# One Strassen chain for the 512 tokens of a block instead of two plain rows and a chain for 256

## The chip, the core and the metric

The kernel runs on one core of a Trainium2 chip. The metric is the device time in microseconds; the times of before are those of 3 runs. All other times here come from one profiled execution.

## What is computed

Attention over 8 batches of 8 heads, 576 positions and 64 channels, with a bias that depends on the distance, and on its output a two-layer block with a snake activation:

```python
scores = scale * np.matmul(q, k.transpose(0, 1, 3, 2)) + bias
attn = softmax(scores)                              # over the last axis
x = np.matmul(attn, v)  # heads side by side: 4608 tokens x 512
h = x @ w_in                                        # 512 -> 2048
s = np.sin(alpha * h)
g = h + s * s / (alpha + 1e-09)
out = g @ w_out                                     # 2048 -> 512, float32
```

## The kernel before

A planner in the kernel's own code orders everything. Each step is a `Task` with the engines that may take it, an assumed duration, its dependencies, a priority and the buffers that it uses; `Plan.run` places the steps one after another by these assumed times and emits their instructions in that order. On the chip each engine then runs its instructions strictly in that order and waits on semaphores for data and for buffers. The planner knows when a step on an engine ends; it does not know how long a store to memory takes: the store is issued inside the step that writes its buffer, and the buffer counts as free when that step ends.

The 4608 tokens are worked in 9 blocks of 512. While batch `t` is in attention (scores and attention outputs on TensorE, exp on ScalarE, the bias as a mask product on VectorE), the second layer of an earlier block is dealt out among its matmuls as filler (`fill`, with the quotas `QUOTA`, `QUOTA1`, `OFFSET`). Then comes the first layer of block `t` (`plan_moe_in`: 64 matmuls of 512 columns; sine on ScalarE, square on ScalarE or VectorE, `g` on VectorE), and then the attention of batch `t + 1`. ScalarE loads a table for exp and one for sine at each change.

The second layer of a block has three forms. Block 0 has four plain rows of 128 tokens (`plan_mo`: 16 matmuls of 512 columns into one bank, a copy to an `outs` buffer and a store of 256 KB). Blocks 1 to 6 have two plain rows and, for the other 256 tokens, a chain (`plan_chain`): a 2 x 2 Strassen product in Winograd's form, with seven products of 8 matmuls of 256 columns, four sums of `g` quarters on VectorE (s1 to s4, in four pieces each; s3 and s4 go to `ss` or over `g` itself) and combined weights in `wsum`. Products share banks by twos. Their results are put together in `outs` by a copy `x` and adds named c11, y, v, w, c22, c21 and c12 after what they make: `take`, line 1389. Blocks 7 and 8 at the end are done by `plan_half`.

Two things matter for what follows. First, buffers: the `outs` tiles are a ring (`NBUF["outs"]`), and a new one may be written only once the store of its last content has landed. PSUM has eight banks: scores and the first layer use 0 to 5, attention outputs (`av`) and second-layer rows and products (`mo`) use 6 and 7. Second, the DMA queues: stores, and the transposes that bring attention outputs to `xT`, are issued by SP in one order; GpSimd issues loads of `v` and, for a batch two later, copies of `k` and `q` in 16 bits to memory (`stage_kq`, from `staged_k` and `staged_q`), which are loaded transposed by SP one block later. Those copies have 576 KB each in small pieces, and `to_stage` puts them at the first layer of blocks 1 to 5.

```python
NBUF = {"ut": 2, "ss": 1, "u": 2, "g": 2, "s16": 3, "sq": 3, "outs": 5, "xn": 6}
BANKS = {"h": (0, 1, 2, 3, 4, 5), "av": (6, 7), "mo": (7, 6), "st": (7, 6, 0, 1, 2, 3, 4, 5)}
```

Of the kernel before, what the change touches and what calls it, by code (L numbers as in the profile page):

```python
# [222 lines left out]

WINDOW = 700
WARM_END = 22.0
QUOTA = 47
QUOTA1 = 28
OFFSET = 0
T_START = 4.0
STEPS = {0: ((1, 1, 1, 1),) * 3, 1: ((3, 1),) * 3}  # L230
T_W0 = 24.5
PRI_S = 0
T_WI = 16.8
# [14 lines left out]
P_ST = 3  # L248
T_TP = ((150, 150), (650, 650), (1500, 1500))
GA = 0.0  # L250
GB = 0.0
GUARD = {"A": GA, "B": GB, "C": 0.0, "X": 0.0}
T_LD = 33.0

AV_AT = (3, 4, 6, 7)
AV_D = (0, 0, 300, 0)
AV_G = (3, 7)
PRE = -100
CUT = 8
RUNS = "aaa c aaa aaa aaa c x aaa abb"  # L260
TAKE = 0
MOEP = (5, 25)
STEP = 700
MIX = "nnssss"
SUMS = {1: (0, 1, 2, 3)}
PACE = ((0, 0), (0, 0), (2, 1), (8, 1))
T_WS = (43.0, 48.3, 48.3, 48.3)
MIX0 = "nnssss"
FIRST = 1
CH = ("mo", "mo", "mo", "st")  # L270
PIECES = 4
AV_LATE = 9900
AV0 = 1500
FILL_GAP = 0.05
# [8 lines left out]
WARM_LAG = 0.3  # L283
WARM_GAP = 0.12
WARM_FROM = 7.3
AV_PRI = 0
NORM_PRI = 200
CP_PRI = 0
SIN_SET = "trig_and_small"
SLACK = {"PE": 0.02, "ACT": 0.02, "DVE": 0.02, "POOL": 0.02, "SP": 0.02}  # L290
# [14 lines left out]
def kernel(  # L305
# [75 lines left out]

    xT = sgl.tile([128, NP, XN], F16, name="xT")
    wsum = sgl.tile([128, 4, NF // 2, DM // 2], F16, name="wsum")
    xv = zz


    natx = tp.tile([128, NF * DM], F16, name="natx", tag="g", bufs=2)
# [26 lines left out]
        return tp.tile([128, DM], F16, name="sq", tag="sq", bufs=NBUF["sq"])  # L414

    def new_ss():
        return tp.tile([128, 6, 512], F16, name="ss", tag="ss", bufs=NBUF["ss"])
# [668 lines left out]
    def plan_moe_in(b, tbl):  # L1086
# [5 lines left out]
        for f in range(NF):  # L1092
# [3 lines left out]
            def mm(e, js, f=f, h=h, hb=hb):  # L1096
                if js[0] == 0:
                    h.v = bank(hb)
                x0 = 512 * b % XN
                m = min(512, XN - x0)  # L1100
                for y, a, n in ((0, x0, m), (m, 0, 512 - m)):
                    if n == 0:
                        continue
                    for j in js:
                        full(h.v[:, y : y + n], w_in16[:, j, 128 * f : 128 * f + 128],
                             xT[:, j, a : a + n], j == 0, j == 3)

            def sn(e, f=f, h=h, s16=s16):
                s16.v = new_s16()
# [52 lines left out]
    def plan_mo(b, a, cut=NF):  # L1162

        mb, ob, m = Buf("mo"), Buf("outs"), Cell()
        for f in range(NF):
            if f == cut:
                yield

            def mm(e, f=f):
                if f == 0:  # L1170
                    m.v = bank(mb)
                full(m.v, gcell[b].v[:, f, 128 * a : 128 * a + 128], w_out16[:, f, :], f == 0, f == NF - 1)

            mo_last[:] = [plan.add({"PE": t_pe(DM)}, mm, mo_last[:] + [gdone[(b, f)]],
                                   500000000 + 4 * b + a, nb=T_WO[f // 4] if b == 0 else 0.0,
                                   new=[mb] if f == 0 else [],
                                   use=[gbuf[b]] if f == 0 else [gbuf[b], mb])]
            mo_last[0].fill = True

        def cp(e):  # L1180
            o = new_outs()
            copy_on(e, o, m.v)
            r0 = 512 * b + 128 * a
            nc.sync.dma_start(out=out[r0 : r0 + 128], in_=o)
# [31 lines left out]
    def plan_half(b, a):  # L1216
# [65 lines left out]
        def add(k, j, to, deps, put=None, first=False, c0=0, c1=n):  # L1282

            def ad(e):
# [2 lines left out]
                    return  # L1287
                cell, i, h = to
                if first:
                    cell.v = new_outs()  # L1290
# [28 lines left out]
    def plan_chain(b, a):  # L1319

        H2, n = NF // 2, DM // 2
        sv, sb = Cell(), Buf("ss")
        bk = [Buf(x) for x in CH]
        bv = [Cell() for _ in range(4)]
        o = Cell(), Cell()
        ob = Buf("outs"), Buf("outs")
        gall = [gdone[(b, f)] for f in range(NF)]
        base = 500000000 + 4 * b + a

        def act(i, j):  # L1330
            return gcell[b].v[:, H2 * j : H2 * j + H2, 128 * (a + i) : 128 * (a + i) + 128]

        def pre(out, x, y, op, deps, first=False):

            made = []
            for h in range(PIECES):
                r = slice(H2 // PIECES * h, H2 // PIECES * (h + 1))

                def sm(e, h=h, r=r):
                    if first and h == 0:  # L1340
                        sv.v = new_ss()
                    nc.vector.tensor_tensor(out=out()[:, r], in0=x()[:, r], in1=y()[:, r], op=op)

                new = first and h == 0
                made.append(plan.add({"DVE": 0.07 + 0.533 / PIECES}, sm, deps + made[-1:], base + PRE, new=[sb] if new else [],
                                     use=[gbuf[b]] if new else [sb, gbuf[b]]))
            return made[-1]

        def sums(k):
            return sv.v[:, 2 * k : 2 * k + 2].rearrange("p k (f t) -> p (k f) t", f=H2 // 2)  # L1350

        def at(k):
            return bv[k // 2].v[:, n * (k % 2) : n * (k % 2) + n]

        def put(i, j):
            if i == 2:
                return xv.bitcast(F32)
            return o[i].v[:, n * j : n * j + n]

        def prod(k, x, w, deps):  # L1360

            for f in range(H2):

                new = f == 0 and k % 2 == 0

                def mm(e, f=f, new=new):
                    if new:
                        bv[k // 2].v = bank(bk[k // 2])
                    full(at(k), x()[:, f], w()[:, f], f == 0, f == H2 - 1)

                mo_last[:] = [plan.add({"PE": t_pe(n)}, mm, mo_last[:] + deps, base,
                                       new=[bk[k // 2]] if new else [],
                                       use=([] if new else [bk[k // 2]]) + [sb, gbuf[b]])]
                mo_last[0].fill = True
                mo_last[0].part = n / DM
                mo_last[0].bank, mo_last[0].reads = bk[k // 2], False
            return mo_last[0]

        def wq(i, j):
# [3 lines left out]
            return lambda: wsum[:, k]  # L1383

        def store(i):
            r = 512 * b + 128 * (a + i)
            nc.sync.dma_start(out=out[r : r + 128, :], in_=o[i].v)

        def take(k, to, x, deps, new=False, last=False):

# [1 line left out]

            def ev(e):
                if new:
                    o[i].v = new_outs()
                if x is None:
                    copy_on(e, put(i, j), at(k))
                else:
                    nc.vector.tensor_tensor(out=put(i, j), in0=at(k), in1=put(*x), op=ALU.add)
                if last:  # L1400
                    store(i)

            bs = [sb] if i == 2 else [] if new else [ob[i]]
            y = plan.add({"DVE": t_dve(n)} if x else {"ACT": t_act(n), "DVE": t_dve(n)}, ev, deps, TAKE,
                         new=[ob[i]] if new else [], use=[bk[k // 2]] + bs)
            y.bank, y.reads = bk[k // 2], True
            return y
# [4 lines left out]
        s4 = pre(lambda: sums(2), lambda: act(0, 1), lambda: sums(1), ALU.subtract, [s2])  # L1412
        p = prod(0, lambda: act(0, 0), wq(0, 0), gall)
        x = take(0, (2, 0), None, [p])
        p = prod(1, lambda: act(0, 1), wq(1, 0), [])
        c11 = take(1, (0, 0), (2, 0), [p, x], True)
        yield
        p = prod(2, lambda: sums(1), ws(1), [s2] + wdone)
        y = take(2, (1, 1), (2, 0), [p, x], True)
        p = prod(3, lambda: act(1, 0), ws(2), [s3])  # L1420
        v = take(3, (1, 0), (1, 1), [p, y])
        yield
        prod(4, lambda: act(1, 1), ws(3), [])
        p = prod(5, lambda: sums(0), ws(0), [])
        w = take(5, (0, 1), (1, 1), [p, y])
        c22 = take(5, (1, 1), (1, 0), [p, v, w])
        take(4, (1, 0), (1, 0), [p, v, c22], last=True)
        yield
        p = prod(6, lambda: sums(2), wq(1, 1), [s4])
        take(6, (0, 1), (0, 1), [p, w, c11], last=True)  # L1430
# [16 lines left out]
    for t in range(T):  # L1447
# [39 lines left out]
            sins += s_  # L1487
        pe_gate = [m]
        if t < T - 1:
            rows = [plan_mo(t, a, CUT if t == 0 and a < 2 else NF) for a in range(2 if t >= FIRST else 4)]  # L1490
            if t == 0 and CUT < NF:
                next(rows[0])
                next(rows[1])
            if t >= FIRST:
                rows, ch = iter(rows), plan_chain(t, 2)
                for x in MIX if t else MIX0:
                    next(next(rows) if x == "n" else ch)
            else:
                for x in rows:
                    next(x)  # L1500
# [38 lines left out]
```

## Time and profile before

| | |
|---|---|
| median of 3 runs | 364.72 us (363.8 to 364.89) |
| profiled execution | 363.98 us, span 362.0 us |
| granted TensorE clock | 0.999 |
| busy: TensorE, ScalarE, VectorE, GpSimd | 356.1, 316.5, 307.0, 93.4 us |
| moved by DMA | 40.53 MB |

The span runs from the first to the last instruction. Busy is the time in which an engine had at least one instruction in work; matmuls overlap in it, so the mean of a matmul's record is longer than the step from one to the next. In rows of a timeline the columns are start, duration, engine, line, operation, what is written from what, shapes and count; in square brackets is the idle time ahead of it and what ended it. SPq is SP's own queue: its rows are the issue of a DMA, not its transfer. Rows of DMA groups give count, size of one and the median time from issue to landing; the answer for one tile and a short window gives the landing of the DMAs issued in it. Of the DMA queues, `software_dynamic` are those that GpSimd issues and `hardware_dynamic` those of SP.

### The profile page before, as it was taken

The numbers are of one execution on the slowest core, as the hardware profiler recorded it, in microseconds if no ns is written. First come the engines' busy times: TensorE is split into PE (matmuls) and PEld (weight loads), VectorE is DVE, ScalarE is ACT, GpSimd is POOL, SyncE is SP. The second block draws the span as 40 slices with busy tenths as digits, with TensorE's granted clock in tenths as the row PEclk, the third lists the DMA queues.
The fourth block names the chain that finished last, engine by engine and source line by source line (L and its number), as shares of the span: only waits on it lengthen the run. The fifth ranks groups of instructions, "written<-read, shape, count | busy, mean of one in ns | idle before, by whom it ended". The sixth has DMA issues, their size and how long they took to land.

```text
span 362.0 us, 9625 instructions
## 1 busy us (share of the span) xinstructions
PE 356.1 (98%) x3812; PEld 218.3 (60%) x3812; DVE 307.0 (85%) x757; ACT 316.5 (87%) x437; POOL 93.4 (26%) x135
## 2 busy tenths in 40 slices
PE   8999999999999999999999999999999999999996
PEld 4564445644575447885684458545787467456685
DVE  4897888989977998699978997899869986999982
ACT  2998999989998999899989999899989998996811
POOL 8578460064000820065001900092006000000000
PEclk9999999999999999999999999999999999999999
DMA  9999999689824996199918992599339422001023
GB/s 169 199 197 183 206 162 144 127 91 123 115 60 104 129 150 109 50 167 140 136 26 167 113 170 51 117 142 144 90 76 151 73 61 53 17 2 59 31 75 102
DMA packets 150157, 40.53 MB, mean 112 GB/s; under 512 B 137224, under 2 KB 145504, under 8 KB 150112
## 3 DMA queue, kind: packets, MB, share of 16 engines
q0 software_dynamic: 96064, 17.67, 60.5%
q1 hardware_dynamic: 53872, 22.16, 25.9%
q8 instruction: 30, 0.49, 0.5%
q10 hardware_dynamic: 176, 0.09, 0.1%
q14 instruction: 15, 0.12, 0.1%
HBM read 37.73 MB, written 16.56 MB: 150 GB/s over the span
## 4 chain that ended last, share of the span: by engine, by line
PE 94%; DMA 2%; DVE 1%; ACT 1%; issue 0%; DVEq 0%; SPq 0%
PE pb L497 92%; DMA m2r<-e_dram 1%; DVE u L779 1%; ACT u L748 1%; DMA e_dram<-e_sb 1%; PE pb L597 1%; PE pb L1066 1%; ACT e_sb L646 0%; PE pb L591 0%; DVE xn L995 0%; ACT xT L578 0%; DVE outs L1292 0%; DVE zz L548 0%; DVE u L765 0%; DVE rd L994 0%
## 5 line engine op out<-in xcount | busy, mean ns | idle before, releaser
L748 ACT ACTIVATE u<-pb 128x1024 f16<-128x1024 f32 (+1 forms) x146 | 136.9, 1018 | 6.3 <-PE pb L497 5.1
L497 PE MATMUL pb<-xT,w_in 128*128 128x512 f16 (+4 forms) x704 | 128.6, 340 | 0.3 <-ACT xT L578 0.3
L1124 DVE SCALAR_TENSOR_TENSOR g<-sq,inv_a,pb 128x512 f16<-128x512 f16 x144 | 101.4, 744 | 3.8 <-ACT sq L1117 1.8
L1110 ACT ACTIVATE s<-pb,alphaT 128x512 f16<-128x512 f32 x144 | 92.9, 693 | 12.4 <-PE pb L497 11.6
L497 PEld LDWEIGHTS <-w_in 128*128 128x128 f16 x704 | 64.4, 98 | 55.5 <-issue 0.5
L497 PE MATMUL pb<-w_out,g 128*128 128x512 f16 (+1 forms) x416 | 83.5, 339 | 0.0
L497 PEld LDWEIGHTS <-g 128*128 128x128 f16 x552 | 50.8, 98 | 34.8 <-issue 5.2
L779 DVE TENSOR_TENSOR u<-u,m2r 128x512 f16<-128x512 f16 (+1 forms) x128 | 61.9, 491 | 9.9 <-ACT u L748 8.5
L497 PEld LDWEIGHTS <-u 128*128 128x128 f16 x1280 | 56.0, 97 | 9.1 <-issue 4.5
L1117 ACT ACTIVATE sq<-s 128x512 f16<-128x512 f16 x76 | 47.5, 640 | 2.0 <-DVE g L1124 1.1
L442 POOL COPY kt<-kT 64x256 f16<-64x256 f16 x12 | 4.9, 406 | 168.9 <-DMA kT<-staged_k 140.6
L497 PE MATMUL pb<-v,u 128*128 128x65 f16 x1024 | 43.9, 193 | 0.0
L497 PE MATMUL pb<-qT,kT 64*128 64x64 f16 (+1 forms) x512 | 42.1, 285 | 0.7 <-DVE qT L580 0.3
L1119 DVE TENSOR_TENSOR sq<-s 128x512 f16<-128x512 f16 x68 | 28.3, 424 | 11.3 <-ACT s L1110 10.3
L995 DVE TENSOR_TENSOR xn<-pb,rd 128x256 f16<-128x256 f32 (+2 forms) x59 | 28.5, 483 | 2.0
L497 PEld LDWEIGHTS <-kT 64*128 64x128 f16 x512 | 17.1, 94 | 20.5 <-issue 13.1
L497 PE MATMUL pb<-vh,u 128*128 128x130 f16 x128 | 28.3, 221 | 0.0
L447 POOL DMA_DIRECT2D v<-in_v_dram x28 | 24.7, 892 | 3.2 <-DMA nat<-in_k_dram 2.2
L1437 ACT ACT_TABLE_LOAD x15 | 19.2, 1283 | 0.3
L748 ACT ACTIVATE nat<-pb 128x1024 f16<-128x1024 f32 (+1 forms) x24 | 18.8, 820 | 0.0
L994 DVE RECIPROCAL rd<-pb 128x4 f32<-128x4 f32 (+2 forms) x59 | 10.9, 185 | 8.1 <-PE pb L497 7.0
L497 PE MATMUL pb<-wsum,g 128*128 128x256 f16 (+1 forms) x136 | 16.7, 267 | 0.0
(96 smaller groups left out, 310.9 us busy)
## 6 DMA issues: line engine op xcount, KB each, us to landing
out_dram<-outs SPq DMA_DIRECT2D x28, 256.0 KB, 2.8
v<-in_v_dram POOLq DMA_DIRECT2D x28, 128.0 KB, 4.7
staged_k<-in_k_dram POOLq DMA_DIRECT2D x6, 576.0 KB, 8.7
staged_q<-in_q_dram POOLq DMA_DIRECT2D x6, 576.0 KB, 12.5
w_in<-in_moe_w_in_dram POOLq DMA_DIRECT2D x4, 512.0 KB, 9.2
w_out<-in_moe_w_out_dram POOLq DMA_DIRECT2D x4, 512.0 KB, 13.6
out_dram<-outs SPq DMA_DIRECT2D x16, 128.0 KB, 1.7
w_out<-in_v_dram SPq DMA_DIRECT2D x6, 128.0 KB, 5.5
```

Source lines behind the costliest of these rows:

```text
L442: nc.gpsimd.tensor_copy(out=kts[t % 2][r, :, r], in_=kTs[t % 2][r, :, 512:S])
L447: nc.gpsimd.dma_start(out=vs[t % 2][:, c, :, 0:D], in_=vp[128 * c : 128 * c + 128],)
L497: nc.tensor.matmul(out=out, lhsT=lhsT, rhs=rhs, start=start, stop=stop, skip_group_check=go_on)
L748: nc.scalar.activation(out=o, in_=x, func=AF.Exp, scale=0.125)
L779: nc.vector.tensor_tensor(out=io, in0=io, in1=m2[:, 2 * p : 2 * p + 2, x0 : x0 + hi - lo], op=ALU.mult)
L994: nc.vector.reciprocal(out=r, in_=x[:, :, :, D])
L995: nc.vector.tensor_tensor(out=xn[:, 0:n].rearrange("p c (z d) -> p c z d", z=2), in0=x[:, :, :, 0:D], in1=r.unsqueeze(3).to_broadcast([128 ...
L1110: nc.scalar.activation(out=s16.v, in_=h.v, func=AF.Sin, scale=alphaT[:, f : f + 1])
L1117: nc.scalar.activation(out=sq.v, in_=s16.v, func=AF.Square)
L1119: k_of(e).tensor_tensor(out=sq.v, in0=s16.v, in1=s16.v, op=ALU.mult)
L1124: nc.vector.scalar_tensor_tensor(out=gcell[b].v[:, f, :], in0=sq.v, scalar=inv_a[:, f : f + 1], in1=h.v, op0=ALU.mult, op1=ALU.add,)
L1437: nc.scalar.preload_act_table_set(name)
```

## The change

- From block 1 to block 6 the second layer is one chain for all 512 tokens: seven products of 16 matmuls of 256 columns, each filling a whole bank (two groups of 128 tokens beside each other). The two plain rows of these blocks go. The order of the products is 0, 1, 2, 3, 5, 4, 6.
- All products take their bank from 6 and 7 (`CH`). The last product is not put into a bank of its own: it is added by TensorE onto the sixth's (`ONTO`), so that the add w falls away.
- The sums are of twice the size, in two pieces instead of four; s4 now overwrites a quarter of `g`. Adds and copies have 512 columns in one instruction (128 x 2 x 256). The copy `x` goes straight into the second half of an `outs` tile.
- An `outs` tile is twice as large and holds 256 tokens, its store has 512 KB, and the ring has 2 tiles instead of 5. `plan_mo` and `plan_half` use half a tile of the same ring. `ss` grows from 6 to 8 pieces.
- The first three feature groups of each block's first layer are split (3, 1) over the four channel groups (`STEPS`); before, only in blocks 0 and 1.
- The planner's quotas, priorities and assumed durations for squares are others.

```diff
-NBUF = {"ut": 2, "ss": 1, "u": 2, "g": 2, "s16": 3, "sq": 3, "outs": 5, "xn": 6}
+NBUF = {"ut": 2, "ss": 1, "u": 2, "g": 2, "s16": 3, "sq": 3, "outs": 2, "xn": 6}
...
-QUOTA = 47
+QUOTA = 34
...
-CH = ("mo", "mo", "mo", "st")
-PIECES = 4
+CH = ("mo",) * 7
+ONTO = True
+ACC = False
+ORD = (0, 1, 2, 3, 5, 4, 6)
+XE = {"ACT": 0.479, "DVE": 0.603}
+PIECES = 2
...
-SQ = {"ACT": 0.51, "DVE": 0.355}
+SQ = {"ACT": 0.45, "DVE": 0.4}
...
     def new_outs():
-        return tp.tile([128, DM], F32, name="outs", tag="outs", bufs=NBUF["outs"])
+        return tp.tile([128, 2 * DM], F32, name="outs", tag="outs", bufs=NBUF["outs"])
...
-        def prod(k, x, w, deps):
+        def prod(k, x, w, deps, onto=None):
 
-            for f in range(H2):
+            z = k if onto is None else onto
+            for f in range(2 * H2):
...
+                    i, g = f // H2, f % H2
+                    full(bv[z].v[:, i], x()[:, g, 128 * i : 128 * i + 128], w()[:, g],
+                         f == 0 and onto is None, f == 2 * H2 - 1, onto is not None)
...
         def store(i):
-            r = 512 * b + 128 * (a + i)
-            nc.sync.dma_start(out=out[r : r + 128, :], in_=o[i].v)
+            r = 512 * b + 256 * i
+            nc.sync.dma_start(out=out[r : r + 256, :].rearrange("(i p) n -> p i n", p=128), in_=o[i].v)
...
+        made = {
+            0: lambda: prod(0, lambda: act(0, 0), wq(0, 0), gall),
+            1: lambda: prod(1, lambda: act(0, 1), wq(1, 0), gall),
...
+            4: lambda: prod(4, lambda: act(1, 1), ws(3), [s1] + wdone),
+            5: lambda: prod(5, lambda: sums(0), ws(0), [s1] + wdone),
+            6: lambda: prod(6, lambda: act(0, 1), wq(1, 1), [d["s4"]] + ([d["c22"]] if ONTO else []), 5 if ONTO else None),
+        }
...
+            ("x", (0,), "", lambda: take(0, (1, 1), None, [p[0]], True)),
...
+            ("c11", (1,), "x", lambda: take(1, (0, 0), (1, 1), [p[1], d["x"]], "y" not in d)),
...
+            ("c21", (4,), "v", lambda: take(4, (1, 0), (1, 0), [p[4], d["v"], d["c22"]], last=True)),
+            ("c12", (6,), "y", lambda: take(5 if ONTO else 6, (0, 1), (0, 1), [p[6], d["w"], d["c11"]], last=True)),
```

Three places show how instructions move. All are at the passage from the first layer of block 3 to the attention of batch 4; lines of the changed kernel have slightly higher numbers.

VectorE before, from the last `g` of block 3 on (`g`: L1124; sums of the chain: L1342; attention output and mask products: L994, L995, L779, L765; row copy: L580):

```order
L1124 SCALAR_TENSOR_TENSOR g<-sq,inv_a,pb 128x512 x3
L1342 TENSOR_TENSOR ss<-g 128x256 x4
L994 RECIPROCAL rd<-pb 128x4
L995 TENSOR_TENSOR xn<-pb,rd 128x256
L779 TENSOR_TENSOR u<-u,m2r 128x2x256
L779 TENSOR_TENSOR u<-u,m2r 128x2x384
L580 COPY outs<-pb 128x512
L779 TENSOR_TENSOR u<-u,m2r 128x2x384
```

VectorE now, from c12 of block 2 (the first row) to c11 of block 3 (the last):

```order
L1398 TENSOR_TENSOR outs<-pb,outs 128x2x256
L1344 TENSOR_TENSOR ss<-g 128x1024
L780 TENSOR_TENSOR u<-u,m2r 128x2x384
L1344 TENSOR_TENSOR ss<-g 128x1024
L766 TENSOR_TENSOR u<-u,mhr 128x2x128
L1344 TENSOR_TENSOR ss<-ss,g 128x1024
L1344 TENSOR_TENSOR g<-g 128x4x256
L1344 TENSOR_TENSOR ss<-ss,g 128x1024
L1344 TENSOR_TENSOR g<-g 128x4x256
L780 TENSOR_TENSOR u<-u,m2r 128x2x256
L1398 TENSOR_TENSOR outs<-pb,outs 128x2x256
```

The row copy is gone; an add that ends a block's last store and the add that writes the next block's first result into the same buffer stand nine rows apart, six of them halves of sums. The add c21 of block 2 stands five rows ahead of the first row shown.

SP before, at the same place (L1387: store of a chain; L965: transposes of the tail of the batch; L1184: store of a row):

```order
L1387 DMA out_dram<-outs 128x512
L965 DMA_TRANSPOSE xT<-xn 128x2x64 x2
L1184 DMA out_dram<-outs 128x512
L1057 DMA_TRANSPOSE xT<-xn 128x3x128
L1184 DMA out_dram<-outs 128x512
```

SP now:

```order
L438 DMA_TRANSPOSE qT_69<-staged_q 128x4x576
L1386 DMA out_dram<-outs 128x2x512
L966 DMA_TRANSPOSE xT<-xn 128x2x64 x2
L1386 DMA out_dram<-outs 128x2x512
L1058 DMA_TRANSPOSE xT<-xn 128x3x128 x2
```

Both stores of a block, of 512 KB each, now stand here, one ahead of the two transposes of the tail and one behind them; the third store is gone.

TensorE before, where the first attention output of batch 4 begins (`vh`, `u`):

```order
L497 LDWEIGHTS g
L497 MATMUL pb<-w_out_79,g 128x512
L497 LDWEIGHTS u
L497 MATMUL pb<-vh_74,u 128x130
```

TensorE now (`wsum`, `ss`: product 2 of the chain, of which nine matmuls stand ahead of it):

```order
L498 LDWEIGHTS ss
L498 MATMUL pb<-wsum,ss 128x256
L498 LDWEIGHTS u
L498 MATMUL pb<-vh_74,u 128x130
```

The attention output stood in the middle of the second plain row, and now it stands in the middle of product 2, behind all of products 0 and 1. On ScalarE the copy `x` of block 3 stands behind six exps of batch 4, where there was no copy of a chain before.

More of the change, by code (lines that the diff above doesn't have):

```diff
@@ L225 @@
 WARM_END = 22.0
-QUOTA = 47
+QUOTA = 34
 QUOTA1 = 28
-OFFSET = 0
+OFFSET = 1
 T_START = 4.0
-STEPS = {0: ((1, 1, 1, 1),) * 3, 1: ((3, 1),) * 3}
+STEPS = {0: ((1, 1, 1, 1),) * 3, **{b: ((3, 1),) * 3 for b in range(1, 8)}}
 T_W0 = 24.5
@@ L1323, in plan_chain @@
         bk = [Buf(x) for x in CH]
-        bv = [Cell() for _ in range(4)]
+        bv = [Cell() for _ in CH]
         o = Cell(), Cell()
@@ L1327, in plan_chain, with pre @@
         gall = [gdone[(b, f)] for f in range(NF)]
-        base = 500000000 + 4 * b + a
+        base = 500000000 + 4 * b
         def act(i, j):
-            return gcell[b].v[:, H2 * j : H2 * j + H2, 128 * (a + i) : 128 * (a + i) + 128]
-        def pre(out, x, y, op, deps, first=False):
+            return gcell[b].v[:, H2 * j : H2 * j + H2, 256 * i : 256 * i + 256]
+        def pre(out, x, y, op, deps, first=False, pieces=PIECES):
             made = []
-            for h in range(PIECES):
-                r = slice(H2 // PIECES * h, H2 // PIECES * (h + 1))
+            for h in range(pieces):
+                r = slice(H2 // pieces * h, H2 // pieces * (h + 1))
                 def sm(e, h=h, r=r):
@@ L1344, in pre @@
                 new = first and h == 0
-                made.append(plan.add({"DVE": 0.07 + 0.533 / PIECES}, sm, deps + made[-1:], base + PRE, new=[sb] if new else [],
+                made.append(plan.add({"DVE": 0.07 + 1.067 / pieces}, sm, deps + made[-1:], base + PRE, new=[sb] if new else [],
                                      use=[gbuf[b]] if new else [sb, gbuf[b]]))
@@ L1394, in ev @@
                 if new:
-                    o[i].v = new_outs()
+                    o[i].v = new_outs().rearrange("p (i n) -> p i n", i=2)
                 if x is None:
-                    copy_on(e, put(i, j), at(k))
+                    copy_on(e, put(i, j), bv[k].v)
                 else:
-                    nc.vector.tensor_tensor(out=put(i, j), in0=at(k), in1=put(*x), op=ALU.add)
+                    nc.vector.tensor_tensor(out=put(i, j), in0=bv[k].v, in1=put(*x), op=ALU.add)
                 if last:
                     store(i)
[L1403 to L1407, printed above, removed]
+            return plan.add({"DVE": t_dve(2 * n)} if x else XE, ev, deps, TAKE,
+                            new=[ob[i]] if new else [], use=[bk[k]] + ([] if new else [ob[i]]) + ([ob[x[0]]] if x and x[0] != i else []))
         s1 = pre(lambda: sums(0), lambda: act(1, 0), lambda: act(1, 1), ALU.add, gall, True)
@@ L1420, in plan_chain @@
[L1420 to L1430, printed above, removed]
+        p, d = {}, {}
@@ new lines, in plan_chain @@
+        acc = None if ACC else 1
+        todo = [
+            ("x", (0,), "", lambda: take(0, (1, 1), None, [p[0]], True)),
+            ("s4", (1,), "", lambda: pre(lambda: act(0, 1), lambda: act(0, 1), lambda: sums(1), ALU.subtract, [s2, p[1]])),
+            ("c11", (1,), "x", lambda: take(1, (0, 0), (1, 1), [p[1], d["x"]], "y" not in d)),
+            ("y", (2,), "x", lambda: take(0 if ACC else 2, (0, 1), acc and (1, 1), [p[2], d["x"]], "c11" not in d)),
+            ("v", (3,), "y", lambda: take(0 if ACC else 3, (1, 0), acc and (0, 1), [p[3], d["y"]])),
+            ("w", (5,), "yv", lambda: d["v"] if ONTO else take(5, (0, 1), (0, 1), [p[5], d["y"], d["v"]])),
+            ("c22", (5,), "vwy", lambda: take(5, (1, 1), (1, 0), [p[5], d["v"], d["w"], d["c11"]])),
+            ("c21", (4,), "v", lambda: take(4, (1, 0), (1, 0), [p[4], d["v"], d["c22"]], last=True)),
+            ("c12", (6,), "y", lambda: take(5 if ONTO else 6, (0, 1), (0, 1), [p[6], d["w"], d["c11"]], last=True)),
+        ]
@@ L1431, in plan_chain @@
+        for k in ORD:
+            p[k] = made[k]()
+            for name, ps, ds, f in todo:
+                if name not in d and all(z in p for z in ps) and all(z in d for z in ds):
+                    if name in ("c22",) and "c11" not in d or name == "c21" and "c22" not in d:
+                        continue
+                    d[name] = f()
+        s4 = d["s4"]
         if to_stage:
@@ L1489 @@
         if t < T - 1:
-            rows = [plan_mo(t, a, CUT if t == 0 and a < 2 else NF) for a in range(2 if t >= FIRST else 4)]
+            rows = [plan_mo(t, a, CUT if t == 0 and a < 2 else NF) for a in range(0 if t >= FIRST else 4)]
             if t == 0 and CUT < NF:
@@ L1494 @@
             if t >= FIRST:
-                rows, ch = iter(rows), plan_chain(t, 2)
-                for x in MIX if t else MIX0:
-                    next(next(rows) if x == "n" else ch)
+                for _ in plan_chain(t):
+                    pass
             else:
```

62 lines of the change are left out of this document (24 added, 38 removed).

## The prediction

> **What bounds the kernel now.** I read the page first, then the busy times of equal stretches, then one passage from block to block on each engine.
>
> ```profile
> PE 356.1 (98%) x3812; PEld 218.3 (60%) x3812; DVE 307.0 (85%) x757; ACT 316.5 (87%) x437; POOL 93.4 (26%) x135
> ...
> PE 94%; DMA 2%; DVE 1%; ACT 1%; issue 0%; DVEq 0%; SPq 0%
> ```
>
> TensorE is busy for 98% of the span and carries 94% of the chain that ended last. Next I asked for two whole periods, each from the last transposes of one batch to those of the next:
>
> ```profile
> core 0: us, PE busy (x) PEld busy (x) DVE busy (x) ACT busy (x) POOL busy (x), PEclk, DMA share, GB/s
> 149.30:188.30 39.00, 39.00 (x477) 28.05 (x475) 33.69 (x86) 36.58 (x49) 10.15 (x11) 1.00 1.04 117
> 188.30:227.20 38.90, 38.90 (x413) 22.77 (x410) 33.79 (x86) 36.58 (x49) 10.35 (x11) 1.00 1.04 118
> ```
>
> TensorE has no gap in them. ScalarE is next with 36.6 of 38.9 us, then VectorE with 33.7. So a matmul less is time less only while ScalarE, VectorE and the DMAs keep pace, and whatever makes TensorE wait is paid in full.
>
> **What is taken from TensorE.** Two plain rows per block (32 matmuls of 512 columns) become 56 more of 256 columns. Matmuls overlap in the record, so I take slopes:
>
> ```profile
> 125.10 2.54 PE L497 MATMUL pb<-w_out,g 128*128 128x512 f16 x11
> ...
> 129.07 0.39 PE L497 MATMUL pb<-w_out,g 128*128 128x512 f16 x1
> ...
> 139.18 0.27 PE L497 MATMUL pb<-w_out,g 128*128 128x256 f16 x1
> ...
> 145.67 1.27 PE L497 MATMUL pb<-wsum,g 128*128 128x256 f16 x10
> ```
>
> (2.54 - 0.39)/10 = 0.215 us for 512 columns, (1.27 - 0.27)/9 = 0.111 for 256. Per block 56 x 0.111 - 32 x 0.215 = 6.22 - 6.88 = -0.66 us, for six blocks -4.0 us. TensorE is the bound, so all of it counts as long as nothing else is late.
>
> **What moves on VectorE and ScalarE.**
>
> ```profile
> L1342 DVE TENSOR_TENSOR ss<-g,ss 128x256 f16<-128x256 f16 x24 | 6.9, 286 | 0.0
> L1243 DVE TENSOR_TENSOR u<-g 128x1024 f16<-128x1024 f16 x8 | 5.4, 686 | 0.0
> L1399 DVE TENSOR_TENSOR outs<-pb,outs 128x256 f32<-128x256 f32 x30 | 12.6, 420 | 1.4 <-PE pb L497 1.2
> L580 DVE COPY outs<-pb 128x512 f32<-128x512 f32 x16 | 11.0, 688 | 0.6 <-PE pb L497 0.3
> L779 DVE TENSOR_TENSOR u<-u,m2r 128x768 f16<-128x768 f16 x64 | 35.2, 552 | 4.7 <-ACT u L748 4.2
> ```
>
> Sums: 16 of 286 ns become 8 of the form that L1243 shows, 686 ns: +0.9 us per block. Evictions: 7 adds and a copy of 256 columns (8 x 0.42 = 3.4) and two row copies (1.4) become 6 adds of 512 columns, which I price like the copy of that size, 0.69: 4.1. Together +0.2 us on an engine with 5 us to spare: nothing.
>
> ```profile
> 167.28 3.77 ACT L748 ACTIVATE u<-pb 128x1024 f16<-128x1024 f32 x4
> ...
> 190.13 0.69 ACT L1110 ACTIVATE s<-pb,alphaT 128x512 f16<-128x512 f32 x1 [1.22 <-PE pb L497]
> ```
>
> The copy `x`, about 0.69 us, goes to ScalarE in five blocks, priced like the sine of that size, which leaves it 2.3 - 0.7 = 1.6 us per period, mostly the 1.2 us that it waits for the first layer; in an undisturbed block that still hides under TensorE. The squares change place, not number; the (3, 1) steps add no matmul. These go at nothing while TensorE stays the bound.
>
> **The stores and their two buffers.** Here I expect the cost. A chain's last two products are computed after the next block's first layer; their adds end in two stores, now of 512 KB, and there are now two `outs` buffers in all. So the next block's `x` (ScalarE) must wait for the first of these stores to land, and its c11 add (VectorE) for the second. Before, with five buffers, nobody asked so soon. In the order SP stands with: store, two transposes of the tail, store. The same place in the trace of before, where the first layer of block 3 ends at 164.05 (below: E):
>
> ```profile
> 164.05 0.27 PE L497 MATMUL pb<-w_out,ss 128*128 128x256 f16 x1
> ...
> 166.63 0.82 PE L497 MATMUL pb<-qT,kT 64*128 64x512 f16 x6
> ...
> 168.12 0.39 PE L497 MATMUL pb<-w_out,g 128*128 128x512 f16 x1
> 168.36 0.59 PE L497 MATMUL pb<-qT,kt 128*128 128x512 f16 x2
> 168.79 2.10 PE L497 MATMUL pb<-w_out,g 128*128 128x512 f16 x9
> ...
> 172.89 0.22 PE L497 MATMUL pb<-vh,u 128*128 128x130 f16 x1
> ...
> 173.89 0.82 PE L497 MATMUL pb<-qT,kT 64*128 64x512 f16 x6
> ```
> ```profile
> 164.91 0.33 SPq L1387 DMA_DIRECT2D out_dram<-outs  x1
> 168.94 2.44 SPq L965 DMA_TRANSPOSE xT<-xn  x2
> 171.47 0.53 SPq L1184 DMA_DIRECT2D out_dram<-outs  x1
> ```
>
> *When c11 is due.* TensorE after E: 24 matmuls of products 4 and 6 (2.7), scores and the tail's products as before (168.12 - 166.63 = 1.5), 1 matmul and two scores (0.5), 7 more end product 6 at E + 5.5. VectorE adds c12 until 6.3, then, in its order, six halves of sums (0.6 each, as they overlap) and three products with the mask (0.55 for the longest, about 1.0 in all): c11 is due at E + 10.9. TensorE meanwhile: 8 + 8 matmuls of product 0, 15 of product 1, two groups of scores (0.75 each), the last of product 1, 9 of product 2, and stands at E + 11.6 before the first attention output. That takes one of the two banks 6 and 7; one holds product 2, the other product 1 until c11 has read it. So from E + 11.6 TensorE waits for c11.
>
> *When its buffer is free.* c12 is ready at 6.3, but SP is held by the two transposes until 171.38, so the store goes out as at 171.47, E + 7.4. How long such a store takes:
>
> ```profile
> L1184 SPq DMA_DIRECT2D out_dram<-outs x1: 530/530/530, 171.5 to 171.5; - x1
> ...
> DMA to landing us min/median/max: 7.2/7.2/7.2
> ```
> ```profile
> L1184 SPq DMA_DIRECT2D out_dram<-outs x1: 534/534/534, 288.2 to 288.2; - x1
> ...
> DMA to landing us min/median/max: 3.2/3.2/3.2
> ```
>
> These two have the same size and the same place behind the two transposes. The first has beside it the copies that GpSimd issues for a later batch, the second (block 6) has none:
>
> ```profile
> 163.11 2.27 POOL L430 DMA_DIRECT2D staged_k<-in_k_dram  x1
> 164.81 2.79 POOL L430 DMA_DIRECT2D staged_q<-in_q_dram  x1
> ```
> ```profile
> staged_k<-in_k_dram POOLq DMA_DIRECT2D x6, 576.0 KB, 8.7
> staged_q<-in_q_dram POOLq DMA_DIRECT2D x6, 576.0 KB, 12.5
> ```
> ```profile
> q0 software_dynamic: 6938, 0.89, 230.8%
> q1 hardware_dynamic: 137, 0.03, 4.3%
> ```
>
> The copies take about 9 and 12 us to land. The last two rows are the queues between 168 and 174: 6,938 packets of the copies, 137 of all that SP had issued. The store goes through when the copies are done. There are six pairs of copies, one for each of the batches 2 to 7; the code puts the last five at the first layers of blocks 1 to 5. A chain's last stores come one block later, so they meet copies after blocks 2, 3, 4 and 5: four times.
>
> Now it is 512 KB, not 256:
>
> ```profile
> out_dram<-outs SPq DMA_DIRECT2D x28, 256.0 KB, 2.8
> ...
> out_dram<-outs SPq DMA_DIRECT2D x16, 128.0 KB, 1.7
> ```
>
> 1.1 us per 128 KB, so between 0 (it queues anyway) and 2.2 us more; I take 1.0. Landing after 7.2 + 1.0 = 8.2 at E + 15.6, less 0.3 since SP no longer has a store (0.33 of issue) ahead of the loads behind which the copies stand; c11 then takes 0.7 and 0.1 to be seen: E + 16.1, 4.5 us after TensorE came. ScalarE's next scores stand behind those attention outputs; without the wait it would need them at about E + 13.4 (first exp at E + 3.2, ten of 0.95 and `x`), with it they come at 16.1 + 1.0 (172.89 to 173.89) + 0.4 = 17.5: 4.1 us. I take 4.1 per passage. Bounds: 2.5 (no dearer than the 256 KB store, copies a microsecond earlier, and some of it caught up) and 5.6 (2.2 for the size). `x` waits for the first store, issued at about E + 3 as the copies begin: due at E + 9, landing near E + 10 to 11. ScalarE loses up to 2 us there, and loses them inside the wait above, not on top.
>
> After block 6, without copies, the store lands 3.2 to 5.4 us after E + 7.4; with c11, 0 to 2 us late: 0.8. The last halves also share two buffers, but their stores land in 1.7 us, TensorE has eight banks there, and a half takes 6 us: 0 to 0.5, I take 0.
>
> **Sum.** 4 x 4.1 + 0.8 - 4.0 = +13.2 us. The profiled execution took 363.98 (span 362.0 and 2.0 around it), which gives 377.2; it lies 0.7 below the median of the runs, 364.72, which gives 377.9. I say 378, with an own range of 4 x 2.5 - 4.4 = +5.6 to 4 x 5.6 + 2.0 - 3.5 = +20.9: 370 to 386. A measurement here tells 0.3% from no change, 1.1 us.
>
> **Rivals.**
> *Stores land in time (faster).* If a store of 512 KB in that place lands within about 3.5 us, c11 finds its buffer free at E + 10.9 and only the matmuls count: 364.7 - 4.0 = 360.7. The point is a landing of 4.3 us: then c11 is done at E + 12.5, five passages cost about 0.8 each and eat the gain. For it: 28 stores have a median of 2.8. Against it: that median mixes stores beside the copies with others, and the one in this very place took 7.2. Chance 0.14. [...]
>
> *The queue is shared, only the size counts (slightly slower).* 2.8 + 2 x 1.1 = 5.0 us, c11 done at E + 13.2, 1.6 us lost in each of five passages: 8 - 4 = +4, 368.7. Chance 0.10.
>
> *ScalarE becomes the bound (about the same).* No store is late, but ScalarE's 36.6 + 0.7 us and its present 1.2 us wait for the first sine leave no more than 0.3 us per block: 364.7 - 6 x 0.3 = 362.9, or no gain if its other short waits stay. Chance 0.06, since a square fewer stands before its table load.
>
> The forecast has 0.70. Slower: 0.70 + 0.10 = 0.80; faster: 0.14 and a third of the last, 0.16; same 0.04. The range 363 to 387 holds some 0.66 of the forecast, the second rival and most of the third.
>
> **What would show it.** In the profile after: ScalarE's copy `outs<-pb` and VectorE's add `outs<-pb,outs` (L1398) with idle time released by DMA `out_dram<-outs`, about 4 us per block on the add, and TensorE idle behind it at an attention output, in the passages after blocks 2 to 5 and hardly after 6; landings of 7 to 9 us for the second store of a block. Periods between blocks near 42.3 us there, near 38.2 where no copies run. If those landings are under 4 us, or VectorE waits for them while TensorE does not, I am wrong, and periods of 38.2 throughout mean 361.

## The result and the profile after

The changed kernel takes 392.02 us (390.11 to 393.99, 4 runs) against 364.71 us on the same chip (363.80 to 364.89): 1.0741 times as long, 95% interval 1.0708 to 1.0775. The prediction was 378, range 363 to 387. The direction was right, the loss twice as large: +27.3 instead of +13.2. The profiled execution took 392.38 us, its span is 390.4.

The page of the changed kernel, busy times and the chain that ended last:

```profile
PE 361.2 (92%) x3956; PEld 234.9 (60%) x3956; DVE 313.5 (80%) x684; ACT 317.9 (81%) x444; POOL 92.6 (24%) x135
...
PE 66%; ACT 12%; DMA 10%; DVE 8%; issue 3%; SPq 1%; ACTq 0%; DVEq 0%
```

TensorE had 94% of the chain, and has 66%. The waits of the whole execution (total, times, longest) name the stores:

```profile
DVE outs L1398 <- DMA out_dram<-outs: 19.8, 4, 5.7
...
PE pb L498 <- DVE outs L1398: 9.2, 4, 3.3
...
ACT outs L579 <- DMA out_dram<-outs: 7.6, 4, 3.0
PE pb L498 <- ACT u L749: 7.4, 5, 2.7
```

Four times VectorE waits for a store (the c11 add), four times ScalarE (`x`), and TensorE waits behind both. The stretches, each cut at a batch's last transposes (columns: window and its length, then the busy time of each engine in the order TensorE, its weight loads, VectorE, ScalarE, GpSimd, the granted clock of TensorE with 1.00 for full speed, DMA share, GB/s):

```profile
0.00:112.00 112.00, 105.38 (x1234) 60.55 (x1235) 92.99 (x231) 98.42 (x134) 46.14 (x82) 0.98 1.09 139
112.00:156.00 44.00, 38.72 (x435) 24.50 (x433) 34.48 (x75) 36.85 (x50) 10.22 (x11) 1.00 0.90 104
156.00:199.70 43.70, 39.05 (x499) 30.23 (x496) 34.55 (x74) 36.78 (x50) 10.13 (x11) 1.00 0.99 105
199.70:244.20 44.50, 40.26 (x436) 25.81 (x434) 34.78 (x74) 36.84 (x50) 10.14 (x11) 0.96 0.97 102
244.20:290.30 46.10, 41.69 (x437) 26.42 (x435) 34.88 (x74) 36.95 (x50) 10.14 (x11) 0.93 0.90 99
290.30:329.20 38.90, 38.79 (x500) 28.70 (x498) 34.61 (x74) 36.84 (x50) 5.79 (x9) 1.00 0.53 87
329.20:390.40 61.20, 57.26 (x446) 38.67 (x443) 47.20 (x88) 35.22 (x66) 0.00 (x0) 1.00 0.17 55
```

The same question to the kernel before, first and last stretch (each of its five periods took 38.9 or 39.0 us):

```profile
0.00:110.40 110.40, 107.44 (x1235) 59.63 (x1236) 91.57 (x241) 99.27 (x135) 46.58 (x82) 1.00 1.13 146
...
305.10:362.00 56.90, 53.97 (x418) 35.98 (x415) 46.83 (x92) 34.32 (x63) 0.00 (x0) 1.00 0.15 50
```

Four periods lose 5 to 7 us each: those with the passages after blocks 2, 3, 4 and 5. The passage after block 6 loses nothing (38.9). Two things were not foreseen: in the last two long periods the granted clock fell (0.96 and 0.93), and the end, without any store wait to speak of, is 4.3 us longer (61.2 against 56.9).

The passage after block 3 in the order of time (E, the end of the first layer of block 3, is 170.37), on SP, ScalarE, TensorE and VectorE:

```profile
175.60 3.21 SPq L966 DMA_TRANSPOSE xT<-xn  x2
178.92 0.52 SPq L1386 DMA_DIRECT2D out_dram<-outs  x1
...
181.68 0.60 ACT L579 ACTIVATE outs<-pb 128x512 f32<-128x512 f32 x1 [2.44 <-DMA out_dram<-outs]
...
183.25 0.39 PE L498 MATMUL pb<-qT,kT 64*128 64x512 f16 x2 [2.33 <-ACT u L749]
...
186.31 0.69 DVE L1398 TENSOR_TENSOR outs<-pb,outs 128x512 f32<-128x512 f32 x1 [4.90 <-DMA out_dram<-outs]
187.05 0.22 PE L498 MATMUL pb<-vh,u 128*128 128x130 f16 x1 [2.22 <-DVE outs L1398]
```

The second store goes out at E + 8.6, behind the two transposes, and takes 7.3 us to land; VectorE had been free since 181.41, E + 11.0; c11 runs at E + 15.9, and the attention output that TensorE stands before starts at E + 16.7.

### The profile page after: what moved, and what is told of

Read it like the earlier page. It is cut to its first block, busy times and chain, and to the rows that moved or that the text cites. A ratio compares the mean times of both kernels' runs of the same rounds, so it can differ in the third digit from the quotient of the medians.

```text
span 390.4 us, 9810 instructions
## 1 busy us (share of the span) xinstructions
PE 361.2 (92%) x3956; PEld 234.9 (60%) x3956; DVE 313.5 (80%) x684; ACT 317.9 (81%) x444; POOL 92.6 (24%) x135
## 4 chain that ended last, share of the span: by engine, by line
PE 66%; ACT 12%; DMA 10%; DVE 8%; issue 3%; SPq 1%; ACTq 0%; DVEq 0%
PE pb L498 65%; DMA out_dram<-outs 7%; ACT u L749 5%; ACT nat L749 2%; ACT s L1112 2%; DVE u L780 2%; DVE ss L1344 2%; ACT sq L1119 2%; DVE outs L1398 1%; DMA m2r<-e_dram 1%; DVE xn L996 1%; DMA phi_sb<-phi_const 1%; PE pb L1067 1%; DMA e_dram<-e_sb 1%; SPq L521 1%
## 5 line engine op out<-in xcount | busy, mean ns | idle before, releaser
L498 PEld LDWEIGHTS <-g 128*128 128x128 f16 x648 | 61.3, 98 | 22.0 <-issue 6.2
L498 PEld LDWEIGHTS <-u 128*128 128x128 f16 x1280 | 58.1, 99 | 15.9 <-issue 12.4
L780 DVE TENSOR_TENSOR u<-u,m2r 128x512 f16<-128x512 f16 (+1 forms) x128 | 59.0, 493 | 7.9 <-ACT u L749 5.1
L498 PE MATMUL pb<-w_out,g 128*128 128x256 f16 (+1 forms) x416 | 59.6, 289 | 0.0
L498 PE MATMUL pb<-qT,kT 64*128 64x64 f16 (+1 forms) x512 | 47.2, 293 | 10.1 <-ACT u L749 7.4
L498 PE MATMUL pb<-v,u 128*128 128x65 f16 x1024 | 45.8, 196 | 0.6 <-DVE u L780 0.6
L1398 DVE TENSOR_TENSOR outs<-pb,outs 128x512 f32<-128x512 f32 x36 | 24.7, 687 | 23.7 <-DMA out_dram<-outs 19.8
L498 PE MATMUL pb<-wsum,g 128*128 128x256 f16 (+1 forms) x232 | 28.9, 271 | 0.8 <-DVE xn L996 0.8
L498 PE MATMUL pb<-wsum,ss 128*128 128x256 f16 x192 | 27.4, 278 | 0.0
L498 PEld LDWEIGHTS <-ss 128*128 128x128 f16 x192 | 17.3, 99 | 5.5 <-issue 3.3
```

The lines of the kernel that those rows point to most:

```text
L498: nc.tensor.matmul(out=out, lhsT=lhsT, rhs=rhs, start=start, stop=stop, skip_group_check=go_on)
L780: nc.vector.tensor_tensor(out=io, in0=io, in1=m2[:, 2 * p : 2 * p + 2, x0 : x0 + hi - lo], op=ALU.mult)
L1398: nc.vector.tensor_tensor(out=put(i, j), in0=bv[k].v, in1=put(*x), op=ALU.add)
```

## The experiments

In all of them the order of instructions on every engine is that of the changed kernel, apart from what the edit names.

**1. Take the waits away, or make the stores fast.** Three buffers instead of two (tables that only the start needs moved into the space of `wsum`):

```
-NBUF = {..., "outs": 2, "xn": 6}
+NBUF = {..., "outs": 3, "xn": 6}
```

> The changed kernel with three outs buffers instead of two (some tables of the start lie in wsum's space to make room; the order on every engine is the same row by row). Theory of the stores: x and c11 find their buffers free, ScalarE and VectorE show no wait for out_dram<-outs, the four periods that took 43.8 to 46.1 us take 38.3 to 38.9, the granted clock stays at 1.00 from 40 us on, and the time is 392.0 less 4 x 5.7 = 369, between 365 and 372. Rival, the order itself costs the time (banks, longer sums on VectorE): the periods stay above 42 us and the time above 383.

369.51 us, 1.0137 (1.0116 to 1.0158): as the theory of the stores said. So 392.02 - 369.51 = 22.5 us of the loss come from the waits and what follows from them, and 4.8 us do not.

The staging copies held back until c11 of the same block's chain is done:

```
+            def later(e):
+                nc.gpsimd.tensor_copy(out=tick, in_=o[0].v[0:1, 0, 0:1])
+                stage_kq(t)
```

> The changed kernel with two buffers, but GpSimd issues each pair of staging copies only once the c11 add of the same block's chain is done (a one-element copy from c11's buffer stands ahead of them). Theory of the stores beside copies: the second store of a block lands 3.2 to 5.4 us after its issue instead of 7 to 8, x does not wait, c11 waits 0 to 2 us, and the time falls to 366 to 376. Rival, the size alone makes the stores slow: they still take over 6 us, and the time stays within 389 to 394.

382.44 us, 1.0497 (1.0453 to 1.0540): 9.6 us less than the changed kernel, though less was gained than expected (366 to 376). The DMA view of 112 to 300 us, first of the changed kernel, then of this one (count, KB, median us from issue to landing):

```profile
out_dram<-outs SPq DMA_DIRECT2D x8, 512.0 KB, 7.3
```
```profile
out_dram<-outs SPq DMA_DIRECT2D x9, 512.0 KB, 2.9
```

The same stores, of the same size, land in 2.9 us when no copies run beside them. So it was the copies, not the size. It stays 12.9 us above the kernel with three buffers. Part of that is a new collision: the copies now meet the transposes of attention outputs that the next first layer needs (median from issue to landing 4.5 us, in the changed kernel 2.4; the waits from 112 to 330 us below). The rest was not taken apart.

```profile
PE pb L498 <- DMA xT<-xn: 7.0, 4, 2.4
...
DVE outs L1398 <- DMA out_dram<-outs: 2.7, 3, 1.1
```

**2. Which of the two waits counts.** First `x` was given a tile of its own (`xv`, and c11 and y read it there).

> The changed kernel with a buffer of its own for x, so that only c11 waits for a store (the first). As predicted, x's wait lies inside c11's: TensorE's wait before the last scores goes (2.3 and 0.9 us in two passages), its wait for c11 grows by as much, and the time stays within 2 us of 392. Rival, the two waits add up: the time falls by x's four waits, 3.0 + 2.4 + 1.0 + 1.1 = 7.5 us, to 383 to 387.

369.56 us, 1.0137 (1.0120 to 1.0154), as with three buffers, and not the 392 that I expected. The expectation says itself that c11 now waits for the first store, and yet gave that wait the price of the second. With `x` gone, c11 is the first of its chain to ask, and by the times it gets the buffer that was let go first, that of the first store; the other is left for v, which comes later. (The trace does not name the buffers; this is inferred from the times.) In the passage after block 3, SP and VectorE:

```profile
172.76 0.88 SPq L1388 DMA_DIRECT2D out_dram<-outs  x1
...
174.79 0.69 DVE L1400 TENSOR_TENSOR outs<-pb,xv 128x512 f32<-128x512 f32 x1
```

c11 runs 2 us after the second store was issued and waits for no DMA. This run therefore does not part the two waits; the next two do, with three buffers bound to the halves of a block:

```
+        tags = "outc", "outs"    # only x waits; "outs", "outc": only c11 waits
+        ob = [Buf(x) for x in tags]
```

> Three buffers, but bound: one for the second half of a block's rows (c21, c22, in which x stands first), two in turn for the first half (c11, c12). So x still waits for the first store of the block before and c11 for none; the order on every engine is that of the changed kernel. If each wait counts for itself: x's four waits, 7.5 us in the changed kernel, stay, and the time is 369.5 + 7.5 = 377 (374 to 379). If x's wait is swallowed by slack on ScalarE: 370 to 372.

377.65 us (372.50 to 379.93), 1.0314 (1.0232 to 1.0396): by the ratios 0.0177 x 364.4 = 6.5 us more than with three buffers. The runs lie far apart: the one of 372.50 had a mean clock of 1.00, those from 377.43 up 0.99, so part of the 6.5 may be the clock.

> The other way round: two buffers in turn for c21 and c22, one for c11 and c12. c11 still waits for the second store and x for none. As predicted (x's wait lies inside c11's): nearly the whole loss stays, 389 to 392. Rival, the two add up: 392.0 - 7.5 = 384.5 or a little less, as the granted clock then falls less (381 to 386).

390.21 us (388.51 to 394.03), 1.0720 (1.0653 to 1.0788): 20.7 us more than with three buffers, although `x` never waits. As predicted, `x`'s wait lies inside c11's: alone it costs 6.5, and on top of c11's by the ratios 0.0021 x 364.4 = 0.8, less than the intervals can tell from nothing. TensorE's single wait is longer here (3.7 to 5.4 us), and in the profiled run the clock falls in all four periods (first and last shown), in that of the changed kernel in two:

```profile
109.30:154.60 45.30, 41.07 (x429) 25.66 (x427) 34.44 (x75) 36.62 (x50) 10.34 (x11) 0.92 0.90 101
...
244.70:291.60 46.90, 41.40 (x432) 26.37 (x432) 34.81 (x74) 36.90 (x50) 10.15 (x11) 0.93 0.93 97
```

That the clock loses more by one long wait is not shown by this. The profiled run was the slowest of this kernel, with a mean clock of 0.969; its other three had 0.978 to 0.982, and the four of the changed kernel 0.972 to 0.982.

**3. The clock.** TensorE of the changed kernel in slices of 3 us, at the two passages after blocks 3 and 5 (window, length, busy time, granted clock, DMA share, GB/s):

```profile
180.00:183.00 3.00, 0.92 (x8) 1.00 2.25 158
183.00:186.00 3.00, 1.59 (x12) 1.00 0.80 193
186.00:189.00 3.00, 1.95 (x35) 1.00 0.01 1
189.00:192.00 3.00, 3.00 (x42) 1.00 0.16 33
...
270.00:273.00 3.00, 1.58 (x12) 1.00 1.13 225
273.00:276.00 3.00, 1.09 (x19) 0.69 0.01 5
276.00:279.00 3.00, 3.00 (x23) 0.50 0.07 15
279.00:282.00 3.00, 3.00 (x22) 0.68 0.10 21
```

The waits behind which the clock fell, after blocks 4 and 5 (the pair of 2.33 and 2.22 us after block 3, behind which it did not, is shown above), and one more place, in the start of the same run:

```profile
230.39 0.27 PE L498 MATMUL pb<-vh,u 128*128 128x130 f16 x1 [3.28 <-DVE outs L1398]
...
274.91 0.27 PE L498 MATMUL pb<-vh,u 128*128 128x130 f16 x1 [3.33 <-DVE outs L1398]
...
20.28 0.28 PE L1067 MATMUL pb<-id_sb,xn 128*128 128x128 f16 x2 [2.06 <-DVE xn L996]
```
```profile
22.00:24.00 2.00, 1.74 (x25) 0.50 1.10 200
```

After the passage behind block 5 TensorE runs for about 9 us at 0.5 to 0.7 of its clock: 3 x (0.31 + 0.50 + 0.32) = 3.4 us lost. Test: matmuls of zeros added where TensorE waits.

```
+                    for _ in range({(1, 14): 8, (2, 8): 20}.get((k, f), 0) if 2 <= b <= 5 else 0):
+                        full(bv[z].v[:, i], zz[:, 0:128], zz[:, 0:n], False, False, True)
```

> The changed kernel with 8 and 20 more matmuls of zeros (256 columns, 0.111 us each: 0.9 and 2.2 us) added onto products 1 and 2 in blocks 2 to 5, at the places where TensorE waits in the four passages; the results are not changed by them. Theory, TensorE's idle time lowers the granted clock afterwards: the clock stays at 1.00 in the fifth and sixth passage, which showed 0.5 to 0.8 for 6 and 9 us, and the time falls by 1.7 + 3.4 = 5 us to 387. Rival, the clock falls for another reason, or the added matmuls stand in the way: 392 to 396.

387.48 us, 1.0636 (1.0618 to 1.0654), at a clock of 1.00 in all four periods: TensorE does 112 matmuls more, VectorE waits as long as before (19.6 us in four waits, against 19.8), and the kernel is 4.5 us faster. So 4.5 of the 22.5 us are the clock, 18.0 the waits themselves (by the ratios 3.8 and 18.2), as far as the added matmuls cost nothing of their own.

**4. What is left, 4.8 us, and where the matmuls' gain went.** All on the kernel with three buffers, whose stretches are (of the four periods the last is shown; they took 38.8, 39.8, 38.9 and 38.8, the second with one 0.9 us wait of VectorE for a store, and a fifth 38.9):

```profile
0.00:111.50 111.50, 106.35 (x1236) 61.10 (x1237) 92.68 (x232) 98.90 (x134) 45.97 (x82) 1.00 1.10 139
...
229.00:267.80 38.80, 38.70 (x438) 25.19 (x436) 34.65 (x74) 36.88 (x50) 10.15 (x11) 1.00 1.12 117
...
306.70:367.90 61.20, 57.24 (x446) 38.63 (x442) 47.23 (x88) 35.22 (x66) 0.00 (x0) 1.00 0.16 55
```

Against before, in the profiled executions (367.9 against 362.0): 1.1 us more up to the first mark, 0.5 in the five periods, 4.3 at the end. An undisturbed period is 0.1 us shorter, not 0.66. Its chain from 229 to 268, against the one of before from 227.2 to 266:

```profile
by line: PE pb L499 81.9%; ACT u L750 9.7%; ACT nat L750 4.7%; DVE xn L997 1.5%; PE pb L1068 1.0%; DVE rd L996 0.5%; DVE nat L794 0.4%; issue 0.4%
```
```profile
by line: PE pb L497 99.8%; PE pb L1066 0.3%
```

The end of the period now runs through ScalarE's last exps and `nat`. I first took ScalarE for the bound and gave `x` to VectorE (`copy_on("DVE", ...)` at the same place):

> The kernel with three buffers, and the copy x done by VectorE at the same place of the program instead of ScalarE; else the same order. Theory, without store waits ScalarE sets the period (36.8 of 38.74 us busy, and it waits only for TensorE's first layer): x's 0.48 us goes from it, the five undisturbed periods fall from 38.8 to about 38.3, TensorE's 0.66 us per block are then seen, and the time is 369.5 - 6 x 0.4 = 367 (366.5 to 368). Rival, TensorE sets the period: 369 to 370.

371.46 us, 1.0188 (1.0142 to 1.0234): not faster, and in the profiled run its four periods are 39.1 to 39.4 us. From 112 to 330 us ScalarE waits 8.1 us for TensorE before an exp, and TensorE for VectorE's adds, which stand among the six halves of sums:

```profile
ACT u L750 <- PE pb L499: 8.1, 15, 0.8
...
PE pb L499 <- DVE outs L1399: 1.2, 4, 0.3
```

Then the other side, 12 matmuls less per block:

```
+                    if 2 <= b <= 5 and k in (1, 2) and 1 <= f <= 6:
+                        return
```

> The kernel with three buffers, where 12 of the 32 matmuls of products 1 and 2 are left out in blocks 2 to 5 (part of the result of these blocks is then missing; the order is else the same). They run in the stretch of the exponentials, as all products of a chain do. 12 x 0.11 = 1.3 us per block, twice the gain that was predicted for the change. Theory: in that stretch ScalarE sets the end (undisturbed periods of 38.8 us against 38.9 before, although TensorE has 0.66 us less to do), so the periods stay at 38.5 to 38.9 and the time at 368.5 to 369.5. Rival, TensorE sets the period: four periods fall to 37.5, the time to 369.5 - 5.3 = 364.

368.64 us, 1.0107 (1.0075 to 1.0138): 0.9 less instead of 5.3, and the interval overlaps that of three buffers. In the stretch of the exps, where these products run, matmuls left out are worth next to nothing; 0.66 us less per block could not bring 4 us. That stretch, from ScalarE's table load for exp to its last `nat`, in the trace of before and then with three buffers (columns as above):

```profile
204.90:226.00 21.10, 21.10 (x303) 13.73 (x302) 17.79 (x55) 20.49 (x22) 2.96 (x2) 1.00 1.14 117
```
```profile
245.20:266.60 21.40, 21.38 (x325) 15.93 (x324) 19.34 (x46) 20.82 (x23) 2.15 (x1) 1.00 1.28 124
```

ScalarE had 0.6 of 21.1 us free there, and it has been given the copy `x`; VectorE had 3.3 and has 2.1. The stretch is 0.3 us longer instead of shorter. But giving `x` to VectorE did not shorten the period, so ScalarE alone is not shown to be the cause; which mixture of the three engines sets the 38.8 us stays open.

The end: behind the last transposes stood 4 matmuls of block 6's chain before, and stand 32 now (its products 4 and 6). 28 x 0.11 = 3.1 us, about the increase of TensorE's busy time there (57.24 - 53.97 = 3.3); the other 1.0 of the 4.3 us is idle time. Leaving 26 of them out:

> The kernel with three buffers, where 26 of the 32 matmuls of the last chain's products 4 and 6 are left out (part of the result of block 6 is then missing; the order is else the same). These products stand behind the last first layer, where before only 4 matmuls of a chain stood. Theory, that end is bound by TensorE and the lag is paid there: 26 x 0.11 = 2.9 us less, 366.6 (366 to 367.2). Rival, the end is bound by ScalarE and VectorE: 368.5 to 369.8.

368.66 us, 1.0125 (1.0078 to 1.0173): in the rival's range, and not to be told from three buffers by the times, so the theory is not borne out. The profile shows why little came back; where the matmuls were, TensorE waits for the adds that follow them:

```profile
326.41 0.49 PE L499 MATMUL pb<-w_out,g 128*128 128x256 f16 x3
329.04 1.03 PE L499 MATMUL pb<-w_out,g 128*128 128x256 f16 x8 [2.13 <-DVE outs L1401]
```

**5. The same space, cut otherwise.** Four buffers of 256 rows by 256 columns, each with a store of its own as soon as it is complete:

```
+            nc.sync.dma_start(
+                out=out[r : r + 256, n * j : n * j + n].rearrange("(i p) n -> p i n", p=128), in_=put(i, j))
...
+            ("c22", (5,), "vwy", lambda: take(5, (1, 1), (1, 0), [...], last=True)),
```

> The changed kernel with the same space for outs, cut otherwise: four buffers of 256 rows by 256 columns instead of two of 256 by 512, each stored by a DMA of its own (256 KB) when its last add is done, so that c11 and c22 go out well before the passage. Theory of the stores: x and c11 find free buffers; the last store (c12) lands about E + 15, where at most y or v waits for it, 0 to 2.5 us each time: 369.5 to 377. Rival, VectorE's wait for a store costs the same wherever it stands in the passage, and SP has more to issue: 385 or more.

367.81 us, 1.0100 (1.0061 to 1.0139), less than the 369.5 to 377 that I expected. No engine waits for a store any more, with the same bytes of buffer; it is the lowest median of the kernels here after the one of before, though not to be told from that with three buffers. It stays 3.6 us behind, of the order of the end in part 4.

## Why the prediction was wrong in size

**Right, step by step.** What was foreseen of the mechanism happened where it was foreseen: four passages, after blocks 2 to 5 and not after 6; VectorE due at E + 10.9 (11.0); the second store held behind the two transposes; slow because of the copies and not of its size; TensorE before the attention output until E + 16.7 (16.1 predicted); `x`'s wait inside c11's. The 0.1 us for c11 to be seen was my estimate; here it is 0.05 (c11 ends at 187.00, the attention output starts at 187.05). The landing was overestimated (8.2, measured 7.3), and the issue underestimated (E + 7.4, measured 8.6, since the two transposes took 3.2 us instead of 2.4 and began 0.3 later); that the two nearly cancel is luck. The term was 17.2 us, and the waits without the clock cost 18.0, all in the four passages: the 0.8 after block 6 did not come (its period is 38.9).

**The faster rival** wanted landings within about 3.5 us. The runs show them where no copies run beside the stores (2.9 us for 512 KB, the median with the copies held back), and not beside the copies (7.3).

**Wrong: the clock was taken as constant (4.5 us).** The step that failed is "whatever makes TensorE wait is paid in full": a wait was priced at its own length, and what runs behind it at full speed. In the trace of before TensorE is full and the clock 1.00 in every period, so no row there showed it; but the sum made it stand for 4 us. What the runs show of it: in the changed kernel the clock fell to 0.50 behind waits of 3.28 and 3.33 us, and stayed at 1.00 behind one of 2.74, after block 2, and behind the pair of 2.33 and 2.22 us with matmuls between; at the start of the same run it fell to 0.50 behind a wait of 2.06 us. With the copies held back it was 0.96 over the period whose longest wait was 1.84 us, and 1.00 over the next, with a wait of 2.35. No threshold follows from these. Before these runs no row told what a wait of 4.1 us costs beyond its length.

**Wrong: the matmul term, -4.0 us (it was +4.8, a difference of 8.8).** Its size per block follows from the slopes, though TensorE's busy time in an undisturbed period fell only from 38.90 to 38.70; the step that failed is "TensorE is the bound, so all of it counts as long as nothing else is late". It was read from whole periods, in which TensorE was full and ScalarE had 2.3 us to spare. But a period has two stretches, and the products run in the one of the exps, where ScalarE had only 0.6 us to spare: there 1.3 us less per block brought next to nothing (experiment 4). The same step put the copy `x` at nothing ("in an undisturbed block that still hides under TensorE"); it went into just that stretch, in six blocks and not five, at 0.60 us. The third rival came nearest, as an alternative to the store waits and with 0.06; something like it holds underneath them as well, but not shown to be ScalarE alone. The rest of the term is the end, 4.3 us in the profiled runs, and the start. At the end the last chain's products lag by 28 matmuls, but 26 of them left out brought back at most some of it, so what sets that end stays open between the matmuls and the adds behind them. I had costed the passages between blocks and taken the tail at 0 by its stores alone, without counting what each engine still has to do behind the last mark, which the order of instructions would have told (TensorE's busy time there rose by 3.3). The first mark itself lies between 109.3 and 112.5 us in profiled runs of kernels whose order up to there is the same (110.1 before), so the 1.1 us are not shown to belong to the change.

Together: 17.2 became 18.0, the clock adds 4.5, and -4.0 became +4.8: 27.3.

## What to carry to other kernels

When work is gathered into larger pieces, count the buffers of what leaves as well: two that are free only after a store has landed put the DMA's worst latency, the one beside other traffic (7.3 us beside the copies here, 2.9 without), onto the chain, and cutting the same bytes by who finishes first took that away. Price a long wait of TensorE above its own length: in the passages here the clock fell behind every wait of 3.28 us or more, and elsewhere behind some of about 2 us too. And price a saving in the stretch where it lies: an engine that is full over a period may be bound by others exactly there, and work taken from it comes back as time only if they have room.

## What the hardware showed that I had not expected

Taking away one of two waits gained next to nothing: without `x`'s wait TensorE stood still for longer in one piece (3.7 to 5.4 us), and the time fell by no more than the runs can tell from nothing, while `x`'s wait alone cost 6.5 us (experiment 2). And 28 useless matmuls per block, put into TensorE's waits, kept the clock at 1.00 and made the kernel 4.5 us faster. How long a wait lowers the clock stays open: one of 2.06 us did, and two of 2.33 and 2.22 us close together did not.
